# Rows of the modulation spread over partitions by DMA transposes instead of TensorE, in an adaptive-LayerNorm block

## The chip, the cores and the metric

The kernel runs on one core of a Trainium2 chip. The core has five engines with instruction streams of their own: TensorE (PE in the profile, its weight loads PEld), VectorE (DVE), ScalarE (ACT), GpSimd (POOL) and SyncE (SP), which here only issues DMAs. ScalarE and GpSimd issue DMAs too; an issue stands in the engine's stream in program order. The metric is the device time of one execution in microseconds, as a median of several runs.

## What is computed

The reference, cut to what matters. Here D = 1024, the sequence is S = 2048, and the feed-forward width is F = 3584; all inputs are bfloat16.

```python
mod = (_silu(c) @ w_mod).reshape(c.shape[0], 6, 1, -1)   # w_mod is 1024 x 6144
sa, ca, ga, sb, cb, gb = (mod[:, 0], ..., mod[:, 5])      # six rows of 1024
h = _layernorm(x) * (1 + ca) + sa
x = x + ga * _A_ref(h, A_wqkv, A_wo)                      # linear attention, 32 heads
h = _layernorm(x) * (1 + cb) + sb
x = x + gb * _B_ref(h, B_w_gate, B_w_up, B_w_down)        # (silu(h @ w_gate) * (h @ w_up)) @ w_down
```

Two of the six rows, sa and ca, are needed at once. The four others are "late": ga scales the output projection w_o, sb and cb modulate the second LayerNorm, gb scales w_down. The kernel multiplies ga into the columns of w_o and gb into the columns of w_down, in SBUF, so for these two it needs the row of 1024 values repeated on all 128 partitions.

## The kernel before

The stages run one after the other on TensorE: K, V and Q projections with the key-value sums (steps ("K", s, i), ("V", s, i), ("Q", s, i) for four chunks s of 512 rows), then 28 gate/up steps for each of the four chunks (("GU", s, f)), with the attention output of the late rows woven into the first pass, then the down projection (("D", st, h)). A list `seq` holds these steps in order; `put(label, ...)` hangs other work behind a step. The order of the program is the order of each engine's stream.

A step of gate/up, and its rotation through five PSUM banks:

```python
def nextbank():
    b = bank[state["b"]]
    state["b"] = (state["b"] + 1) % 5
    return b

def gu_mm(sc_, f):
    ...
    g_ps = nextbank()
    for cc in range(DC):                       # 8 matmuls of 512 columns
        nc.tensor.matmul(g_ps[:], lhsT=wg_blk[:, cc, fs], rhs=M4[:, sc_, cc, :], ...)
    sg = epool.tile([P, NB], F32, name="e")
    nc.scalar.activation(out=sg[:], in_=g_ps[:], func=ACT.Silu)
    u_ps = nextbank()
    for cc in range(DC):
        nc.tensor.matmul(u_ps[:], lhsT=wu_blk[:, cc, fs], rhs=M4[:, sc_, cc, :], ...)
    nc.vector.tensor_tensor(out=gus[sc_][:, f, :], in0=u_ps[:], in1=sg[:], op=ALU.mult)
```

Weight blocks of gate and up (512 KB each, two steps' worth) come on SyncE's queue into three buffers. During the first pass ScalarE's queue carries the transposes of the attention output and of the normalised rows:

```python
def nd_tr(st):
    nc.scalar.dma_start_transpose(out=oTs[st % 3], in_=os_[st % 2])
def o_tr(st):
    nc.scalar.dma_start_transpose(out=M4[:, sc_, :, t * P:(t + 1) * P], in_=xn2s[st % 3])
```

The late rows ga, cb and sb are made thus: eight transposing loads of w_mod, so that the 1024 columns of a row lie on partitions (128 at a time); eight multiply-and-sum instructions on VectorE against silu(c) spread over all partitions (`sc_bc`); each gives 128 values in one column of `colF`.

```python
def load_late(q, i, js):
    for j in js:
        nc.sync.dma_start_transpose(out=rowT[i][:, j], in_=wm_v[:, j, q * D:(q + 1) * D])
def late_sum(q, i, bs):
    for b in bs:
        nc.vector.tensor_tensor_reduce(out=prod..., in0=rowT[i][:, :, b, :], in1=sc_bc..., ...,
                                       accum_out=colF[:, q, b:b + 1])
```

A result in columns must be turned back into a row on all partitions for silu(c) and for ga: VectorE repeats each column 128 times along the free dimension (`spread`, into `rep`), then TensorE transposes the eight squares and ScalarE copies them out of PSUM:

```python
def late_bc(dst):
    tp = nextbank()[:].bitcast(BF16).rearrange("p (c s) -> p c s", c=DC)
    for cc in range(DC):
        nc.tensor.transpose(tp[:, cc, :], rep[:, cc, :], ident[:])
    nc.scalar.copy(out=dst[:].rearrange("p (c s) -> p c s", c=DC), in_=tp)
```

The row gb is made in another way. Two plain loads bring its part of w_mod in halves of 512 columns; VectorE sums eight slices, weighted by silu(c) as a scalar per partition, splits the float32 sum into two bfloat16 parts, and TensorE sums over partitions with a square of ones, which leaves the row on all partitions at once (`part_sum`, `part_split`, `part_bc`).

Of the kernel before, what the change touches and what calls it, by code (L numbers as in the profile page):

```python
# [9 lines left out]
ALU = mybir.AluOpType  # L10
BF16 = mybir.dt.bfloat16
F32 = mybir.dt.float32
# [9 lines left out]
def kernel(  # L22
# [13 lines left out]
    nc = tc.nc  # L36
    P = nc.NUM_PARTITIONS
    _, S, D = A_x.shape
# [3 lines left out]
    DC = D // P  # L42
# [5 lines left out]
    NB = 512  # L48
    NH = D // NB
    FC = F // P  # L50
# [16 lines left out]
    wm_v = w_mod.rearrange("(p j) n -> p j n", j=DC)  # L67
    c_v = c.rearrange("o (p j) -> p (o j)", j=DC)

    const = ctx.enter_context(tc.tile_pool(name="const", bufs=1))  # L70
# [10 lines left out]
    M3 = const.tile([P, 16384], BF16, name="M3")  # L81
# [5 lines left out]
    def view(region, off, shape, dtype=BF16):  # L87
        n = 1
        for s_ in shape:
            n *= s_  # L90
        w = n * (2 if dtype == F32 else 1)
        ap = region[:, off:off + w]
        if dtype == F32:
            ap = ap.bitcast(F32)
        if len(shape) == 2:
            ap = ap.rearrange("p (a b) -> p a b", a=shape[0])
        elif len(shape) == 3:
            ap = ap.rearrange("p (a b c) -> p a b c", a=shape[0], b=shape[1])
        return ap
# [19 lines left out]
    obs = [view(M6, 4096 + 1024 * i, [D]) for i in range(2)]  # L119
    rowT = [view(M3, 4096, [DC, DC, P]), view(M6, 0, [DC, DC, P])]  # L120
    prod = view(M5, 8256, [D], F32)
    wmg = [view(M3, 4096 * (1 + i), [DC, NB]) for i in range(2)]
    accG = view(M3, 12288, [D], F32)
    hlG = view(M3, 14336, [2, NB])
    xs = [view(M7, 1024 * i, [D]) for i in range(6)]
    xns = [view(M7, 6144 + 1024 * i, [D]) for i in range(6)]
    wgs = [view(M7, 4096 * i, [DC, FBW]) for i in range(3)]
# [2 lines left out]
    def wd(f):  # L130
        return wd_lo[:, f] if f < 14 else wd_hi[:, f - 14]
# [40 lines left out]
    ident = const.tile([P, P], BF16, name="ident")  # L172
# [11 lines left out]
    ga_bc = const.tile([P, D], BF16, name="ga_bc")  # L184
    gb_bc = ga_bc
    KVZ = const.tile([P, HG, KVW], BF16, name="KVZ")
    rep = const.tile([P, DC, P], BF16, name="rep")
    sc_bc = const.tile([P, D], BF16, name="sc_bc")
    colF = const.tile([P, 6, DC], F32, name="colF")
    ones = const.tile([P, P], BF16, name="ones")  # L190
    nc.gpsimd.memset(ones[:], 1.0)
    scF = const.tile([P, DC], F32, name="scF")

    scT = const.tile([P, DC], BF16, name="scT")
    nc.scalar.activation(out=scT[:], in_=c_sb[:], func=ACT.Silu)
    nc.scalar.copy(out=scF[:], in_=scT[:])

    def warm(n):
        for _ in range(n):
# [62 lines left out]
# [4 lines that stand above are left out]
# [54 lines left out]
    GA, SB, CB, GB = 2, 3, 4, 5  # L320

    def load_late(q, i, js):
        for j in js:
            nc.sync.dma_start_transpose(out=rowT[i][:, j], in_=wm_v[:, j, q * D:(q + 1) * D])

    def late_sum(q, i, bs):
        for b in bs:
            nc.vector.tensor_tensor_reduce(out=prod.rearrange("p (j k) -> p j k", j=DC), in0=rowT[i][:, :, b, :],  # L328
                                           in1=sc_bc[:].rearrange("p (j k) -> p j k", j=DC), scale=1.0, scalar=0.0,
                                           op0=ALU.mult, op1=ALU.add, accum_out=colF[:, q, b:b + 1])  # L330

    def late_fin(q):
        if q == SB:
            nc.vector.tensor_copy(out=sbT[:], in_=colF[:, q, :])
        else:
            nc.vector.tensor_copy(out=m1[:, q, :], in_=colF[:, q, :])
            if q == CB:
                nc.vector.tensor_scalar_add(out=cb1T[:], in0=m1[:, q, :], scalar1=1.0)
            else:
                spread(nc.vector, m1[:, q, :])  # L340
# [1 line left out]
    def spread(eng, col):  # L342
        eng.tensor_copy(out=rep[:], in_=col.unsqueeze(2).to_broadcast([P, DC, P]))

    def late_bc(dst):
        tp = nextbank()[:].bitcast(BF16).rearrange("p (c s) -> p c s", c=DC)
        for cc in range(DC):
            nc.tensor.transpose(tp[:, cc, :], rep[:, cc, :], ident[:])  # L348
        nc.scalar.copy(out=dst[:].rearrange("p (c s) -> p c s", c=DC), in_=tp)

    def load_gb(kb):
        k0 = GB * D + kb * NB
        nc.sync.dma_start(out=wmg[kb], in_=wm_v[:, :, k0:k0 + NB])

    def part_sum(kb, js):
        dst = accG[:, kb * NB:(kb + 1) * NB]
        for j in js:
            if j == 0:
                nc.vector.tensor_scalar_mul(out=dst, in0=wmg[kb][:, 0, :], scalar1=scF[:, 0:1])
            else:  # L360
                nc.vector.scalar_tensor_tensor(out=dst, in0=wmg[kb][:, j, :], scalar=scF[:, j:j + 1], in1=dst,  # L361
                                         op0=ALU.mult, op1=ALU.add)

    def part_split(kb):
        src = accG[:, kb * NB:(kb + 1) * NB]
        nc.vector.tensor_copy(out=hlG[:, 0, :], in_=src)
        nc.vector.tensor_tensor(out=hlG[:, 1, :], in0=src, in1=hlG[:, 0, :], op=ALU.subtract)

    def part_bc(kb):
        b = nextbank()  # L370
        for s_ in range(2):
            nc.tensor.matmul(b[:], lhsT=ones[:], rhs=hlG[:, s_, :], start=(s_ == 0), stop=(s_ == 1))
        nc.scalar.copy(out=gb_bc[:, kb * NB:(kb + 1) * NB], in_=b[:])


    def tr0(st):
# [113 lines left out]
    def put(label, *fns):  # L490
        after.setdefault(label, []).extend(fns)
# [156 lines left out]
    put(("K", 1, 7), lambda: [load_x(st) for st in range(12, 16)])  # L648


    put(("V", 0, 5), lambda: late_bc(sc_bc))

    def put_late(q, i, loads, sums):
        for k in range(DC):
            put(loads[k], lambda k=k: load_late(q, i, (k,)))
            put(sums[k], lambda k=k: late_sum(q, i, (k,)))
        put(sums[-1], lambda: late_fin(q))

    put_late(GA, 0, [("Q", 0, k) for k in range(8)], [("V", 1, k) for k in range(8)])
    put(("K", 2, 3), lambda: late_bc(ga_bc))  # L660
    put_late(CB, 1, [("V", 1, k) for k in range(8)], [("V", 2, k) for k in range(8)])
    put(("V", 2, 7), lambda: nc.sync.dma_start(out=wo, in_=wo_v))
    put_late(SB, 0, [("V", 2, k) for k in range(8)], [("V", 3, k) for k in range(8)])
    put(("GU", 0, 18), lambda: load_gb(0), lambda: load_gb(1))
    gb_at = [("GU", 0, f) for f in range(21, FC)] + [("GU", 1, f) for f in range(8)]
    for kb in range(2):
        for k in range(4):
            put(gb_at[5 * kb + k], lambda kb=kb, k=k: part_sum(kb, (2 * k, 2 * k + 1)))
        put(gb_at[5 * kb + 3], lambda kb=kb: part_split(kb))
        put(gb_at[5 * kb + 5], lambda kb=kb: part_bc(kb))  # L670
    for cc in range(DC):
        put(("K", 3, 4 + cc) if cc < 4 else ("V", 3, cc - 4), lambda cc=cc: nc.vector.tensor_tensor(out=wo[:, cc, :], in0=wo[:, cc, :], in1=ga_bc[:],
                                                               op=ALU.mult))
# [41 lines left out]
            range(14 + 4 * (i - 4), min(18 + 4 * (i - 4), FC)) for i in range(8)}  # L715
    for i in range(8):
        for k, f in enumerate(wd_f[i]):
            put(("GU", 1, max(3 * i + 4, 7 + i) + k // 2) if i < 7 else ("GU", 1, FC - 2 + k),
                lambda f=f: nc.vector.tensor_tensor(out=wd(f), in0=wd(f), in1=gb_bc[:], op=ALU.mult))
    put(("GU", 1, FC - 4), lambda: load_x1r(0), lambda: load_x1r(1))  # L720
    for st in range(2, ST):
# [37 lines left out]
```

## Time and profile before

| quantity | value |
|---|---|
| time, median of 3 runs | 840.07 us (839.58 to 840.27) |
| span of the profiled execution | 837.9 us |
| busy: TensorE, VectorE, ScalarE, GpSimd | 827.3, 354.6, 153.2, 79.5 us |
| granted TensorE clock | 1.000 |
| bytes moved by DMA | 128.62 MB |
| transposing DMAs | 32 on ScalarE's queue, 36 on SyncE's |

How to read it: a group's line gives the source line, engine, operation, output and input with shapes, the number of instructions, then busy time, the mean of one in ns, and the idle time of the engine just before. The program's big SBUF regions all appear as M, the PSUM banks as bank; gb_bc is the same memory as ga_bc and bears its name. A windows line gives the stretch, its length, then busy time of PE, PEld, DVE, ACT and POOL with instruction counts, the granted clock, the mean busy share of the 16 DMA engines (over 1 where packets overlap) and GB/s. A timeline line gives start, length, engine, source line and operation; a trailing q on an engine (SPq, ACTq) means its instruction sequencer, as in the issue of a DMA. Busy times of TensorE overlap one another, since its matmuls are pipelined.

### The profile page before, as it was taken

How to read it: one execution, taken by the hardware profiler on the slowest of the kernel's cores; microseconds unless marked ns; L12 is line 12 of the kernel's file. 1: busy time of each engine (PE TensorE's matmuls, PEld its weight loads, DVE VectorE, ACT ScalarE, POOL GpSimd, SP SyncE). 2: the span in 40 equal slices, each digit the busy share in tenths (PEclk: the TensorE clock that was granted, in tenths of full speed). 3: DMA queues.
4: the chain of work that ended last, by engine and by line, in shares of the span. 5: the costliest groups of instructions: out<-in, count | busy, mean ns of one | idle time of the engine just before them, and what ended most of it. 6: DMA issues, size and time to landing. Idle time of an engine off the chain costs nothing.

```text
span 837.9 us, 10535 instructions
## 1 busy us (share of the span) xinstructions
PE 827.3 (99%) x4148; PEld 390.2 (47%) x4228; DVE 354.6 (42%) x662; ACT 153.2 (18%) x289; POOL 79.5 (9%) x147
## 2 busy tenths in 40 slices
PE   8999999999999999999999999999999999999998
PEld 4454544544444444444444444444444444444445
DVE  5758888788656656635342111112101111111111
ACT  3335533323211111111110001111000111100000
POOL 2114300032222223100000000000000000000000
PEclk9999999999999999999999999999999999999999
DMA  9985878154598999787884225555312555211220
GB/s 300 312 180 111 130 175 202 41 136 125 146 216 219 224 231 283 189 251 226 251 248 136 76 70 151 154 153 154 104 70 90 155 152 152 75 37 45 76 70 26
DMA packets 220993, 128.62 MB, mean 154 GB/s; under 512 B 76048, under 2 KB 207120, under 8 KB 220944
## 3 DMA queue, kind: packets, MB, share of 16 engines
q1 hardware_dynamic: 180096, 98.58, 42.9%
q10 hardware_dynamic: 38544, 20.98, 10.9%
q0 software_dynamic: 2304, 8.39, 2.6%
q8 instruction: 33, 0.54, 0.3%
q14 instruction: 16, 0.13, 0.1%
HBM read 97.52 MB, written 12.58 MB: 131 GB/s over the span
## 4 chain that ended last, share of the span: by engine, by line
PE 96%; SPq 2%; DMA 1%; issue 1%; DVE 0%; DVEq 0%
PE bank L576 23%; PE bank L595 23%; PE bank L570 23%; PE bank L527 7%; PE bank L289 7%; PE bank L297 7%; PE bank L274 6%; DMA M<-in_w_mod_dram 1%; PE bank L500 1%; PE bank L306 1%; SPq L147 1%; SPq L150 1%; SPq L140 0%; PE bank L348 0%; DVE M L361 0%
## 5 line engine op out<-in xcount | busy, mean ns | idle before, releaser
L576 PE MATMUL bank<-M,M 128*128 128x512 bf16 x881 | 210.4, 379 | 0.9
L570 PE MATMUL bank<-M,M 128*128 128x512 bf16 x870 | 209.5, 379 | 1.3
L578 DVE TENSOR_TENSOR M<-bank,e 128x512 bf16<-128x512 f32 x112 | 77.4, 691 | 249.8 <-PE bank L576 241.3
L595 PE MATMUL bank<-M,M 128*128 128x512 bf16 (+2 forms) x717 | 147.4, 362 | 0.7
L573 ACT ACTIVATE e<-bank 128x512 f32<-128x512 f32 x112 | 66.8, 598 | 436.2 <-PE bank L570 404.1
L595 PEld LDWEIGHTS <-M 128*128 128x128 bf16 x952 | 90.9, 98 | 103.0
L576 PEld LDWEIGHTS <-M 128*128 128x128 bf16 x896 | 87.7, 98 | 105.7
L570 PEld LDWEIGHTS <-M 128*128 128x128 bf16 x896 | 87.3, 98 | 103.8
L598 DVE TENSOR_TENSOR M<-bank,M 128x512 bf16<-128x512 f32 (+2 forms) x34 | 22.4, 660 | 169.9 <-PE bank L595 169.9
L274 PE MATMUL bank<-M,M 128*128 128x512 bf16 x248 | 56.6, 379 | 1.7 <-DVE M L256 1.0
L527 PE MATMUL bank<-M,M 128*128 128x512 bf16 x254 | 57.8, 379 | 0.1
L297 PE MATMUL bank<-M,M 128*128 128x512 bf16 x250 | 56.7, 379 | 0.3
L289 PE MATMUL bank<-M,M 128*128 128x512 bf16 x251 | 55.8, 379 | 0.3
L269 ACT ACTIVATE e<-bank 128x512 f32<-128x512 f32 x64 | 37.7, 595 | 86.1 <-PE bank L297 49.6
L595 PE MATMUL bank<-M 128*128 128x512 bf16 x218 | 50.3, 379 | 0.2
L271 DVE SCALAR_TENSOR_TENSOR M<-bank,e 128x512 bf16<-128x512 f32 x64 | 44.3, 691 | 3.9
L270 DVE TENSOR_SCALAR e<-e 128x512 f32<-128x512 f32 x64 | 29.4, 460 | 24.9 <-ACT e L269 24.9
L289 PEld LDWEIGHTS <-M 128*128 128x128 bf16 x256 | 25.0, 98 | 30.0
L527 PEld LDWEIGHTS <-M 128*128 128x128 bf16 x256 | 25.0, 98 | 29.7
L274 PEld LDWEIGHTS <-M 128*128 128x128 bf16 x256 | 24.3, 98 | 29.3 <-DVE M L256 1.8
L297 PEld LDWEIGHTS <-M 128*128 128x128 bf16 x256 | 24.6, 98 | 27.9
L328 DVE CUSTOM_DVE_ANT_0 M<-M,sc_bc 128x1024 f32<-128x1024 bf16 x24 | 29.8, 1241 | 0.5
(85 smaller groups left out, 358.2 us busy)
## 6 DMA issues: line engine op xcount, KB each, us to landing
M<-in_B_w_gate_dram SPq DMA_DIRECT2D x56, 512.0 KB, 3.8
M<-in_B_w_up_dram SPq DMA_DIRECT2D x56, 512.0 KB, 4.9
x_scratch<-M POOLq DMA_DIRECT2D x16, 512.0 KB, 5.6
M<-x_scratch ACTq DMA_DIRECT2D x16, 512.0 KB, 3.4
M<-in_B_w_down_dram SPq DMA_DIRECT2D x6, 1024.0 KB, 8.2
M<-in_A_x_dram SPq DMA_DIRECT2D x16, 256.0 KB, 3.9
M<-in_A_wqkv_dram SPq DMA_DIRECT2D x4, 1024.0 KB, 11.4
M<-in_A_x_dram ACTq DMA_DIRECT2D x16, 256.0 KB, 3.8
```

The costliest lines, as they stand in the source:

```text
L269: nc.scalar.activation(out=e[:], in_=acc, func=ACT.Exp)
L271: nc.vector.scalar_tensor_tensor(out=dst, in0=acc, scalar=0.0, in1=e[:], op0=ALU.max, op1=ALU.add)
L274: nc.tensor.matmul(acc[:], lhsT=M4[:, sc_, cc, t * P:(t + 1) * P], rhs=wk[:, cc, h * NB:(h + 1) * NB], start=(cc == 0), stop=(cc == DC - 1))
L289: nc.tensor.matmul(acc[:], lhsT=M4[:, sc_, cc, t * P:(t + 1) * P], rhs=wv[:, cc, h * NB:(h + 1) * NB], start=(cc == 0), stop=(cc == DC - 1))
L297: nc.tensor.matmul(acc[:], lhsT=wq[:, cc, qc * P:(qc + 1) * P], rhs=M4[:, sc_, cc, :], start=(cc == 0), stop=(cc == DC - 1))
L328: nc.vector.tensor_tensor_reduce(out=prod.rearrange("p (j k) -> p j k", j=DC), in0=rowT[i][:, :, b, :], in1=sc_bc[:].rearrange("p (j k) -> ...
L527: nc.tensor.matmul(acc[:], lhsT=oTs[st % 3][:, cc, :], rhs=wo[:, cc, hs], start=(cc == 0), stop=(cc == DC - 1))
L570: nc.tensor.matmul(g_ps[:], lhsT=wg_blk[:, cc, fs], rhs=M4[:, sc_, cc, :], start=(cc == 0), stop=(cc == DC - 1))
L573: nc.scalar.activation(out=sg[:], in_=g_ps[:], func=ACT.Silu)
L576: nc.tensor.matmul(u_ps[:], lhsT=wu_blk[:, cc, fs], rhs=M4[:, sc_, cc, :], start=(cc == 0), stop=(cc == DC - 1))
L578: nc.vector.tensor_tensor(out=gus[sc_][:, f, :], in0=u_ps[:], in1=sg[:], op=ALU.mult)
L595: nc.tensor.matmul(y_ps[:, 0:w], lhsT=gus[sc_][:, f, t * P:(t + 1) * P], rhs=wd(f)[:, c0:c1], start=(f == 0), stop=(f == FC - 1))
```

## The change

Everything that spread rows over partitions by TensorE is done by DMA. `late_bc` becomes a single transposing DMA from `rep` to the destination, SBUF to SBUF, issued by SyncE for silu(c) and ga. The special path of gb goes: gb is now made like the three other late rows, but its eight transposing loads and its spreading are issued on ScalarE's queue, where the transposes of that stage already are. The scaling of w_down by gb moves to later steps of the second gate/up pass, since gb is ready later. The purpose is to free TensorE, PSUM banks and ScalarE's evictions from the work of spreading rows, and to have one way for all late rows.

The diff, cut to its core (`...` marks cuts; the removed buffers wmg, accG, hlG, ones and scF served only the removed path):

```diff
-    ones = const.tile([P, P], BF16, name="ones")
-    nc.gpsimd.memset(ones[:], 1.0)
-    scF = const.tile([P, DC], F32, name="scF")
...
-    nc.scalar.copy(out=scF[:], in_=scT[:])
...
     def load_late(q, i, js):
+        eng = nc.scalar if q == GB else nc.sync
         for j in js:
-            nc.sync.dma_start_transpose(out=rowT[i][:, j], in_=wm_v[:, j, q * D:(q + 1) * D])
+            eng.dma_start_transpose(out=rowT[i][:, j], in_=wm_v[:, j, q * D:(q + 1) * D])
...
-    def late_bc(dst):
-        tp = nextbank()[:].bitcast(BF16).rearrange("p (c s) -> p c s", c=DC)
-        for cc in range(DC):
-            nc.tensor.transpose(tp[:, cc, :], rep[:, cc, :], ident[:])
-        nc.scalar.copy(out=dst[:].rearrange("p (c s) -> p c s", c=DC), in_=tp)
-
-    def load_gb(kb):
-        k0 = GB * D + kb * NB
-        nc.sync.dma_start(out=wmg[kb], in_=wm_v[:, :, k0:k0 + NB])
-
-    def part_sum(kb, js):
-        dst = accG[:, kb * NB:(kb + 1) * NB]
-        for j in js:
-            ...        # 8 multiply-adds of 128x512 on VectorE, by scF[:, j:j + 1]
-    def part_split(kb):
-        ...            # a bfloat16 copy and the rest, on VectorE
-    def part_bc(kb):
-        b = nextbank()
-        for s_ in range(2):
-            nc.tensor.matmul(b[:], lhsT=ones[:], rhs=hlG[:, s_, :], start=(s_ == 0), stop=(s_ == 1))
-        nc.scalar.copy(out=gb_bc[:, kb * NB:(kb + 1) * NB], in_=b[:])
+    def late_bc(eng, dst):
+        eng.dma_start_transpose(out=dst[:].rearrange("p (c s) -> p c s", c=DC),
+                                in_=rep[:].rearrange("p c s -> p (c s)"))
...
-    put(("V", 0, 5), lambda: late_bc(sc_bc))
+    put(("V", 0, 5), lambda: late_bc(nc.sync, sc_bc))
...
-    put(("K", 2, 3), lambda: late_bc(ga_bc))
+    put(("K", 2, 3), lambda: late_bc(nc.sync, ga_bc))
...
-    put(("GU", 0, 18), lambda: load_gb(0), lambda: load_gb(1))
-    gb_at = [("GU", 0, f) for f in range(21, FC)] + [("GU", 1, f) for f in range(8)]
-    for kb in range(2):
-        ...            # part_sum, part_split, part_bc put at gb_at[5 * kb + k]
+    put_late(GB, 0, [("GU", 0, 22 + k) if k < 6 else ("GU", 1, k - 6) for k in range(8)], [("GU", 1, 2 + k) for k in range(8)])
+    put(("GU", 1, 10), lambda: late_bc(nc.scalar, gb_bc))
...
-            put(("GU", 1, max(3 * i + 4, 7 + i) + k // 2) if i < 7 else ("GU", 1, FC - 2 + k),
+            put(("GU", 1, (12, 14, 16, 18, 19, 21, 23)[i] + k // 2) if i < 7 else ("GU", 1, FC - 2 + k),
                 lambda f=f: nc.vector.tensor_tensor(out=wd(f), in0=wd(f), in1=gb_bc[:], op=ALU.mult))
```

More of the change, by code (lines that the diff above doesn't have):

```diff
@@ L121 @@
     prod = view(M5, 8256, [D], F32)
-    wmg = [view(M3, 4096 * (1 + i), [DC, NB]) for i in range(2)]
-    accG = view(M3, 12288, [D], F32)
-    hlG = view(M3, 14336, [2, NB])
     xs = [view(M7, 1024 * i, [D]) for i in range(6)]
@@ L343, in spread @@
         eng.tensor_copy(out=rep[:], in_=col.unsqueeze(2).to_broadcast([P, DC, P]))
-    def late_bc(dst):
-        tp = nextbank()[:].bitcast(BF16).rearrange("p (c s) -> p c s", c=DC)
-        for cc in range(DC):
-            nc.tensor.transpose(tp[:, cc, :], rep[:, cc, :], ident[:])
-        nc.scalar.copy(out=dst[:].rearrange("p (c s) -> p c s", c=DC), in_=tp)
-    def load_gb(kb):
-        k0 = GB * D + kb * NB
-        nc.sync.dma_start(out=wmg[kb], in_=wm_v[:, :, k0:k0 + NB])
-    def part_sum(kb, js):
-        dst = accG[:, kb * NB:(kb + 1) * NB]
-        for j in js:
[L358 to L362, printed above, removed]
-    def part_split(kb):
-        src = accG[:, kb * NB:(kb + 1) * NB]
-        nc.vector.tensor_copy(out=hlG[:, 0, :], in_=src)
-        nc.vector.tensor_tensor(out=hlG[:, 1, :], in0=src, in1=hlG[:, 0, :], op=ALU.subtract)
-    def part_bc(kb):
-        b = nextbank()
-        for s_ in range(2):
-            nc.tensor.matmul(b[:], lhsT=ones[:], rhs=hlG[:, s_, :], start=(s_ == 0), stop=(s_ == 1))
-        nc.scalar.copy(out=gb_bc[:, kb * NB:(kb + 1) * NB], in_=b[:])
+    def late_bc(eng, dst):
+        eng.dma_start_transpose(out=dst[:].rearrange("p (c s) -> p c s", c=DC),
+                                in_=rep[:].rearrange("p c s -> p (c s)"))
     def tr0(st):
@@ L663 @@
     put_late(SB, 0, [("V", 2, k) for k in range(8)], [("V", 3, k) for k in range(8)])
-    put(("GU", 0, 18), lambda: load_gb(0), lambda: load_gb(1))
-    gb_at = [("GU", 0, f) for f in range(21, FC)] + [("GU", 1, f) for f in range(8)]
-    for kb in range(2):
[L667 to L670, printed above, removed]
+    put_late(GB, 0, [("GU", 0, 22 + k) if k < 6 else ("GU", 1, k - 6) for k in range(8)], [("GU", 1, 2 + k) for k in range(8)])
+    put(("GU", 1, 10), lambda: late_bc(nc.scalar, gb_bc))
     for cc in range(DC):
```

## Prediction

> **What bounds the kernel now.** I read the page from the top: the busy shares, then the chain of work that ended last, then TensorE's busy time in three long stretches of the windows view.
>
> ```profile
> PE 827.3 (99%) x4148; PEld 390.2 (47%) x4228; DVE 354.6 (42%) x662; ACT 153.2 (18%) x289; POOL 79.5 (9%) x147
> ...
> PE 96%; SPq 2%; DMA 1%; issue 1%; DVE 0%; DVEq 0%
> ...
> 0.00:24.00 24.00, 20.71 (x211) 11.12 (x215) 11.59 (x34) 7.25 (x8) 5.41 (x27) 1.00 0.97 308
> 24.00:448.00 424.00, 421.46 (x2132) 200.66 (x2171) 280.56 (x536) 112.45 (x225) 74.05 (x120) 1.00 0.76 194
> 448.00:838.00 390.00, 385.16 (x1814) 178.39 (x1847) 62.45 (x92) 33.48 (x56) 0.00 (x0) 1.00 0.33 100
> ```
>
> The first line says that TensorE is busy 99% of the span, the second that 96% of the closing chain is TensorE work. A busy share alone would not settle it, since matmuls overlap in the record. The Trainium skill, "Perfetto Trace Analysis", section "Identifying the Most-Contended Engine", warns of just that and points to the weight loads instead; here weight loads are busy only 47%, so that number alone would suggest slack. The pitch of the matmuls decides: eight matmuls of a bank start 1.73 us apart from the next eight in the timeline of the gate/up stage, 0.216 us each, for 512 columns, over and over, at a granted clock of 1.00. And when I ask the waits view for TensorE alone, from 25 us to the end, it lists no wait at all. Only the first 24 us have gaps (20.71 of 24.00 us busy), where the chain runs through the first loads of w_mod and wqkv. So after 24 us **the instruction stream of TensorE is the time**: what is taken out of it shortens the run by its slot, and what is done on another engine costs nothing until TensorE must wait for it.
>
> **What the change takes out of TensorE.** The timeline shows the slots. What counts is the start of the group's first weight load to the start of the next group's, not the durations.
>
> ```profile
> 41.00 0.65 PEld L348 LDWEIGHTS <-rep 128*128 128x128 bf16 x8
> ...
> 41.61 2.31 PEld L289 LDWEIGHTS <-M 128*128 128x128 bf16 x12
> ...
> 364.40 0.31 PEld L372 LDWEIGHTS <-ones 128*128 128x128 bf16 x2
> ...
> 364.83 1.61 PEld L570 LDWEIGHTS <-M 128*128 128x128 bf16 x8
> ```
>
> Eight transposes of rep hold TensorE from 41.00 to 41.61: 0.61 us. The second spreading, at 96.88 to 97.49, is the same 0.61. The two matmuls against ones for one half of gb hold it from 364.40 to 364.83: 0.43 us, and the other half from 346.70 to 347.13 too. In all 2 x 0.61 + 2 x 0.43 = **2.08 us**. The Trainium skill has a figure for the transposes ("TensorE: Matmul & The Clock Gate", section "Part 4: PE-mode transpose": about 390 ns in isolation, about 275 ns within a kernel). Sixteen by that would be 4.4 to 6.2 us; the trace gives 219 ns for one and a pitch of 76 ns in the run of eight, so I use the trace.
>
> **What else goes and comes.** ScalarE loses two evictions of 1.02 us and two of 0.585 us (3.2 us), VectorE the partial sums of gb: 14 x 0.747 + 2 x 0.476 + 2 x 0.426 + 2 x 0.693 = 13.7 us. VectorE gains eight sums of 128x1024 at 1.24 + 0.08 us, one column copy (0.17) and one spread of rep (0.69): 11.4 us. Both lie beside TensorE. The ones memset and the scF copy (0.20 us each) lie at 1.32 and 4.05 us on POOL and ScalarE; POOL then idles 2.78 us for VectorE, and ScalarE 2.16 us for POOL, so neither is on the way. The scaling of w_down keeps its 28 x 0.68 us of VectorE and only moves to later slots, still inside the second gate/up pass, while the first w_down matmul stands at about 448 us.
>
> The two big plain loads of w_mod (2 x 1 MB at 305.7 us, 10.6 and 15.0 us to landing) go. In their place ScalarE's queue issues eight transposing loads of 256 KB, one per gate/up step from step 22 of the first pass (about 326 to 360 us), and one spreading. SyncE's queue gets two spreadings. What such a load costs is seen where the earlier rows are loaded by SyncE:
>
> ```profile
> 50.33 12.06 SPq L324 DMA_TRANSPOSE M<-in_w_mod_dram  x8
> ...
> 52.00:56.00 4.00, 3.95 (x20) 1.77 (x19) 3.29 (x9) 1.43 (x3) 0.00 (x0) 1.00 1.00 222
> 56.00:60.00 4.00, 4.00 (x20) 1.86 (x19) 3.93 (x10) 1.55 (x3) 0.00 (x0) 1.00 0.95 179
> ...
> L324 SPq DMA_TRANSPOSE M<-in_w_mod_dram x24: 1232/1308/4452, 50.3 to 120.9; - x24
> ...
> DMA to landing us min/median/max: 3.9/4.3/9.1
> ```
>
> Eight take 12.06 us of issue with the DMA engines full (the last columns of a windows line are clock, DMA share and GB/s), so each is about 1.5 us of all DMA engines, and holds its issuing engine 1.3 us as a rule and 4.45 us at worst. The Trainium skill ("DMA: Bandwidth & Descriptors", section "Issuing engines are not separate DMA queues") says that the issuing engine saves only issue time and that all queues share 16 DMA engines; so ScalarE's queue buys order against the other transposes on that queue, not bandwidth. The section "Silent corruption: two transposing streams in flight at once" of the same page of the Trainium skill asks that one queue's transposes wait for the other's. That would be a wait, but SyncE's last transpose is issued at 120.9 and landed by 130 us, and ScalarE's first is at 161.3 us; the new spreadings on SyncE (41 and 97 us) and the gb loads on ScalarE keep this split.
>
> On SyncE the first spreading stands behind four transposes of x and ahead of plain loads, 1.23 us of issue like its neighbours; the sums that need it begin at 77 us, 30 us later. The second stands between two transposes of x at about 100 us; w_o is scaled with it some 30 us later. Both hidden.
>
> **Rivals.** First, *ScalarE is held up by issuing*. One gate/up step is 3.45 us and ScalarE has one activation of 0.60 us in it, so 2.85 us are free. At 1.3 us per issue this fits twice; at 4.6 us, as one transpose in the saturated stretch took, it doesn't:
>
> ```profile
> 310.27 4.61 ACTq L546 DMA_TRANSPOSE M<-M  x1
> ...
> 340.00:344.00 4.00, 4.00 (x20) 1.86 (x19) 3.49 (x6) 0.60 (x1) 0.00 (x0) 1.00 1.10 273
> 344.00:348.00 4.00, 4.00 (x21) 1.77 (x19) 1.24 (x3) 1.05 (x2) 0.00 (x0) 1.00 0.78 218
> 348.00:352.00 4.00, 3.95 (x19) 1.86 (x19) 3.96 (x11) 0.73 (x2) 0.00 (x0) 1.00 0.42 112
> ```
>
> TensorE turns through five banks, 1.73 us a group, so a bank comes back four groups, 6.9 us, after it is full; less 0.6 us of eviction, about 6.3 us of lateness are free, and the 4.61 us issue above cost TensorE nothing. If all eight took 4.6 us, each would be 1.75 us over its step: 14 us of lateness, about 8 us lost. But the DMA share from 340 to 356 us is 0.42 to 1.10, mean 0.71, and eight loads at 1.5 us per 3.45 us add 0.43: near full, not beyond the 1.16 seen at 320 to 332 us with no wait of TensorE. I give a visible stall one chance in eight, typically 1 to 4 us.
>
> Second, *VectorE waits for a landing*. Each gb sum reads all eight loads; the last is issued after the activation of step 1 of the second pass, near 358 us, and with 4.3 to 9.1 us to landing arrives at 362 to 367 us, beside 1 MB of w_down. The first sum stands behind the product at 362 us: a wait of 0 to 5 us against about 6.2 us free. Likewise the last transposed tile of the hidden rows now queues behind three gb loads; in the kernel before, it was issued at 338.5 and used at 349 us. Probably hidden.
>
> Third, *the weights come late*: gate and up blocks of 1 MB per 6.9 us land in 3.8 to 4.9 us at the median, and are asked for two blocks (13.8 us) ahead. Landing would have to triple. Removing the two 1 MB loads even eases 305 to 324 us. Against it.
>
> Fourth, *a gain beyond the slots*, were the DMA or VectorE a hidden limit now: the empty list of TensorE waits speaks against it.
>
> **Range and chances.** 840.07 - 2.08 = 838.0 us, a ratio of 0.9975. Runs of the kernel before spread 0.7 us. Downward I allow that and a little: 837.2. Upward, one stall of 1.5 to 2 us eats the gain: 839.8. Two per cent is 16.8 us, twice the whole-backlog case, so nearly all chance is within it.
>
> **What would show it.** Right: TensorE has 20 fewer instructions and the gate/up, Q/K/V and down stages keep their pitch; the span falls by about 2 us, half of it by 100 us and half by 365 us; TensorE still lists no wait after 25 us; the issues on ScalarE's queue take 1.3 to 3 us. Wrong: TensorE waits for activations or products between 326 and 395 us, with issues of 4 us or more (first rival); VectorE idle until a w_mod landing (second); a weight-load wait for gate or up blocks (third); or a changed opening before 24 us, which my sum leaves untouched.

## The result and the profile after

The changed kernel takes 837.89 us (median of 6 runs, 837.63 to 838.31) against 840.1 us for the kernel before in the same series, a ratio of 0.9973 with a 95% interval of [0.996, 0.9986]. It was measured again later, beside one of the experiments: 838.12 against 839.81 us, 0.9977 [0.9967, 0.9986]. So the gain is about 2 us, and it is there.

The page of the changed kernel, its busy shares and the engines of the chain that ended last, and then the windows view of the two long stretches behind the opening (columns: stretch, its length, busy time of PE, PEld, DVE, ACT and POOL, clock, DMA share, GB/s):

```profile
PE 829.2 (99%) x4208; PEld 388.7 (46%) x4208; DVE 351.3 (42%) x660; ACT 149.9 (18%) x284; POOL 79.2 (9%) x146
...
PE 97%; SPq 2%; DMA 1%; issue 0%; DVE 0%
```

```profile
24.00:446.00 422.00, 421.68 (x2152) 199.25 (x2149) 277.20 (x534) 109.42 (x221) 74.06 (x120) 1.00 0.78 196
446.00:836.00 390.00, 387.23 (x1850) 178.49 (x1848) 62.44 (x92) 33.43 (x56) 0.00 (x0) 1.00 0.34 100
```

The picture has not changed: TensorE is the chain, and its waits view from 25 us to the end is as empty as before. One trap lies in the first line. TensorE's busy time went *up*, 827.3 to 829.2 us, though it has 20 instructions less to do. The weight loads tell the truth: 4228 became 4208, exactly 20 fewer. The matmul records of the kernel before were incomplete (its gate matmuls are listed as 870, the changed kernel's as 896, which is 112 groups of eight), and where records are missing, the busy time is too small. A busy time with records missing can't judge a gain of 2 us.

A better ruler is the distance between two marks that both kernels have: the first weight load of a V projection in the opening, and the first of the down projection. Here are the two marks in the kernel before and in the changed kernel, each from the view of one source line (durations min/median/max in ns, then first and last start in us):

```profile
L289 PEld LDWEIGHTS <-M x256: 97/98/98, 30.6 to 147.3; 128*128 128x128 bf16 x128
L595 PEld LDWEIGHTS <-M x952: 97/98/98, 447.7 to 834.7; 128*128 128x128 bf16 x191
```

```profile
L282 PEld LDWEIGHTS <-M x256: 97/98/98, 30.6 to 146.4; 128*128 128x128 bf16 x128
L563 PEld LDWEIGHTS <-M x952: 97/98/98, 445.9 to 833.0; 128*128 128x128 bf16 x191
```

From 30.6 to 447.7 us is 417.1 us before; from 30.6 to 445.9 us is 415.3 us after: **1.8 us** less. The last weight load of the V projections, at 147.3 against 146.4 us, splits it: 0.9 us by then, where only the two spreadings differ, and another 0.9 us by the second mark, where only gb differs. In what follows this distance is called the stretch; the marks are given to 0.1 us.

### The profile page after: what moved, and what is told of

Same layout as the page of the kernel before. It is cut to its first block, busy times and chain, and to the rows that moved or that the text cites. A ratio compares the mean times of both kernels' runs of the same rounds, so it can differ in the third digit from the quotient of the medians.

```text
span 836.1 us, 10576 instructions
## 1 busy us (share of the span) xinstructions
PE 829.2 (99%) x4208; PEld 388.7 (46%) x4208; DVE 351.3 (42%) x660; ACT 149.9 (18%) x284; POOL 79.2 (9%) x146
## 4 chain that ended last, share of the span: by engine, by line
PE 97%; SPq 2%; DMA 1%; issue 0%; DVE 0%
PE bank L563 23%; PE bank L538 23%; PE bank L544 23%; PE bank L282 7%; PE bank L495 7%; PE bank L290 7%; PE bank L267 6%; DMA M<-in_w_mod_dram 1%; SPq L144 1%; PE bank L468 1%; PE bank L299 1%; SPq L147 0%; SPq L137 0%; PE bank L363 0%; DVE M L566 0%
## 5 line engine op out<-in xcount | busy, mean ns | idle before, releaser
L322 DVE CUSTOM_DVE_ANT_0 M<-M,sc_bc 128x1024 f32<-128x1024 bf16 x32 | 40.0, 1249 | 0.5
L282 PEld LDWEIGHTS <-M 128*128 128x128 bf16 x256 | 25.0, 98 | 30.2
```

Of the source, the lines that this page charges most:

```text
L282: nc.tensor.matmul(acc[:], lhsT=M4[:, sc_, cc, t * P:(t + 1) * P], rhs=wv[:, cc, h * NB:(h + 1) * NB], start=(cc == 0), stop=(cc == DC - 1))
```

## The experiments

Three theories stood behind the expectations. Theory A: TensorE's stream is the time, and what an instruction costs there is read from the start of one group's matmuls to the start of the next's. Theory B: the same, with slots read from the weight loads, as the prediction did. Theory C: the gain comes from relief of the DMA engines or VectorE on the new path of gb. All stretches found:

| kernel | marks, us | stretch | time, us | ratio to before [95%] |
|---|---|---|---|---|
| before | 30.6, 447.7 | 417.1 | 840.07 | |
| changed | 30.6, 445.9 | 415.3 | 837.89 | 0.9973 [0.996, 0.9986] |
| spreadings only | 32.6, 448.8 | 416.2 | 838.94 | 0.9987 [0.9979, 0.9995] |
| gb only | 30.2, 446.4 | 416.2 | 839.08 | 0.9988 [0.998, 0.9996] |
| spreadings eightfold on TensorE | 30.3, 453.6 | 423.3 | 846.39 | 1.0073 [1.0059, 1.0088] |
| gb loads two a step | 30.8, 449.2 | 418.4 | 838.67 | 0.9989 [0.9976, 1.0001] |
| gb loads all at once | 30.6, 458.5 | 427.9 | 849.96 | 1.0114 [1.0097, 1.0131] |
| gb on SyncE's queue | 30.9, 451.5 | 420.6 | 839.67 | 1.0005 [0.9994, 1.0017] |
| opening filled | 30.5, 445.9 | 415.4 | 838.04 | 0.9978 [0.9968, 0.9987] |
| changed, again | 31.2, 446.5 | 415.3 | 838.12 | 0.9977 [0.9967, 0.9986] |

Marks and stretch are of the one profiled execution, the time is the median of all, and each ratio is to runs of the kernel before in the same series.

### The two spreadings alone

```diff
 (the kernel before, with)
-    def late_bc(dst):   # eight TensorE transposes and a ScalarE copy
+    def late_bc(eng, dst):   # one transposing DMA
-    put(("V", 0, 5), lambda: late_bc(sc_bc))
+    put(("V", 0, 5), lambda: late_bc(nc.sync, sc_bc))
-    put(("K", 2, 3), lambda: late_bc(ga_bc))
+    put(("K", 2, 3), lambda: late_bc(nc.sync, ga_bc))
```

> The kernel before, with only the two spreadings of silu(c) and ga done by DMA; gb keeps its ones matmuls. Theory A (the time is TensorE's stream, and a slot is read from matmul start to matmul start: 41.22 to 41.66 us, 0.44 us for eight transposes): the first w_down weight load, at 447.7 us before and 445.9 in the changed kernel, comes 0.9 us earlier than before (446.8), time 839.2. Theory B (slots read from weight loads, 0.61 us each, as predicted): 1.2 us earlier. Theory C (the gain is relief of DMA or VectorE by the new gb path): no gain at all here, 0 to 0.2 us.

The time was 838.94 us, 0.9 us below the 839.83 us of before in this series. In the profiled execution everything came 2 us late from the opening on (the clock was halved there; the last section shows it), so the bare position of the second mark says nothing and the stretch has to be taken: 416.2 us, 0.9 us below before. That is theory A's number, and theory C's nothing is out. Against theory B's 1.2 us speaks the stretch alone, with marks given to 0.1 us; the interval of the ratio, a gain of 0.4 to 1.8 us, holds both.

### gb alone

```diff
 (the changed kernel, with TensorE's late_bc kept as pe_bc)
-    put(("V", 0, 5), lambda: late_bc(nc.sync, sc_bc))
+    put(("V", 0, 5), lambda: pe_bc(sc_bc))
-    put(("K", 2, 3), lambda: late_bc(nc.sync, ga_bc))
+    put(("K", 2, 3), lambda: pe_bc(ga_bc))
```

> The changed kernel with the two spreadings put back on TensorE; only gb goes the new way. Theory A: the first w_down weight load comes 0.86 us earlier than before (446.8 to 446.9 us), and together with the run that has the spreadings alone it makes up the whole 1.8 us. Theory B also says 0.86 here. Theory C: nearly the whole 1.8 us is found here.

839.08 us, 0.75 us below before. The second mark came at 446.4 us, but the first came 0.4 us early as well; the stretch is 416.2 us, again 0.9 us shorter. The two halves add up: 0.9 + 0.9 = 1.8 us, the whole of the change. Within the 0.1 us to which the marks are given, nothing is left over for an interaction of the two, or for theory C.

### The spreadings eightfold

```diff
 (the kernel before, with)
     def late_bc(dst):
         ...
-        for cc in range(DC):
+        for cc in list(range(DC)) * 8:
             nc.tensor.transpose(tp[:, cc, :], rep[:, cc, :], ident[:])
```

> The kernel before, with each of the two spreadings' eight transposes done eight times over into the same bank (14 times eight more than before, the row is the same). Theory A (0.44 us per eight): 14 x 0.44 = 6.2 us more than before, 846.3 us. Theory B (0.61 us per eight): 14 x 0.61 = 8.5 us, 848.6 us. If TensorE's stream were not the time (theory C), much less than 6 us would show.

This magnifies the disputed term. The time was 846.39 us against 839.83, 6.6 us more; the interval of the ratio, 0.59% to 0.88%, is 5.0 to 7.4 us and leaves theory B's 8.5 us out. The stretch grew by 6.2 us (423.3 - 417.1) for 14 additional groups: **0.443 us for eight transposes**, 55 ns each. So one more TensorE transpose in this stream costs 55 ns. It isn't the 219 ns of its record, and not the 76 ns that the weight loads of one short run suggested. TensorE's timeline shows where the 76 came from; here are the weight loads, then the matmuls, of the first group of 64:

```profile
40.66 3.77 PEld L348 LDWEIGHTS <-rep 128*128 128x128 bf16 x64
44.40 3.17 PEld L289 LDWEIGHTS <-M 128*128 128x128 bf16 x16
...
40.88 3.74 PE L348 MATMUL bank<-ident,rep 128*128 128x128 bf16 x64
44.45 3.62 PE L289 MATMUL bank<-M,M 128*128 128x512 bf16 x15
```

By the weight loads the group takes 44.40 - 40.66 = 3.74 us, by the matmuls 44.45 - 40.88 = 3.57 us. The difference is 0.17 us, the same as for eight (0.61 against 0.44). So the weight loads are wrong by a fixed amount per group, which spread over only eight transposes looks like a dearer transpose. The eightfold run alone gives the cost of each further transpose; that nothing fixed comes on top for a whole group is shown by the run with the spreadings alone, 0.9 us for two.

### Bunching the gb loads on ScalarE

The first rival of the prediction was that ScalarE, held up by issuing loads, is late with its activations until TensorE has no free bank. In the changed kernel that didn't happen. Two kernels push it there: two loads a step, and all eight at once.

```diff
 (the changed kernel; gb loads, two a step)
-    put_late(GB, 0, [("GU", 0, 22 + k) if k < 6 else ("GU", 1, k - 6) for k in range(8)], ...)
+    put_late(GB, 0, [("GU", 0, 25 + k // 2) if k < 6 else ("GU", 1, 0) for k in range(8)], ...)
 (all at once)
+    put_late(GB, 0, [("GU", 0, 25) for k in range(8)], ...)
```

> The changed kernel with the eight gb loads bunched, two in each of four gate/up steps (25 to 27 of the first pass and 0 of the second) instead of one in each of eight. At 1.9 us an issue, the median in the changed kernel, two take 3.8 us against 2.85 us that ScalarE has free in a step: 0.95 us late per step, some 4 us after four, inside the 6.3 us that five banks allow: no wait of TensorE, 837.9 us. If issues slow to 4 us because the DMA engines are full, 5 us late per step, some 20 us after four: TensorE loses 10 us or more, about 850 us. I expect the middle: 0 to 3 us lost.

> The changed kernel with all eight gb loads issued one after the other behind step 25 of the first gate/up pass. SyncE issued eight such loads in 12 to 13 us earlier in the kernel, with little else on the DMA engines; here the gate and up weights run beside them, so 13 to 20 us. ScalarE does no activation in that time. If ScalarE's issuing only costs once lateness passes the slack of the banks, 6.3 us less what it had: TensorE stalls 7 to 14 us, and the time is 845 to 852 us. If ScalarE's lateness never reaches TensorE (the slack is larger than I think): 837.9. If every us of issue counts: 13 to 20 us more than the changed kernel.

All at once first. The timeline of ScalarE, then of TensorE, with the windows of that time (clock, DMA share and GB/s in the last three columns):

```profile
341.80 0.60 ACT L541 ACTIVATE e<-bank 128x512 f32<-128x512 f32 x1 [2.86 <-PE bank L538]
341.80 18.80 ACTq L318 DMA_TRANSPOSE M<-in_w_mod_dram  x8
360.70 1.57 ACT L541 ACTIVATE e<-bank 128x512 f32<-128x512 f32 x3 [18.30 <-DMA M<-in_w_mod_dram]
...
361.35 3.57 PE L544 MATMUL bank<-M,M 128*128 128x512 bf16 x8 [9.23 <-ACT e L541]
364.71 2.69 PE L538 MATMUL bank<-M,M 128*128 128x512 bf16 x8
...
356.00:360.00 4.00, 0.00 (x0) 0.00 (x0) 0.00 (x0) 0.00 (x0) 0.00 (x0) 0.51 1.23 270
360.00:364.00 4.00, 2.65 (x7) 0.98 (x7) 2.67 (x8) 1.57 (x3) 0.00 (x0) 0.50 0.60 118
364.00:368.00 4.00, 4.00 (x15) 1.53 (x14) 1.82 (x4) 0.56 (x1) 0.00 (x0) 0.71 0.00 0
```

The issues hold ScalarE for 18.80 us. The next activation was due one step of 3.45 us after 341.80, at 345.25, and began at 360.70: 15.45 us late. TensorE stood for 9.23 us. The difference, **6.2 us**, is the lateness that five banks absorb; the prediction had worked out 6.3. The three activations at once at 360.70 are the backlog. The stretch is 12.6 us longer than the changed kernel's, and the starts of the groups split that. 0.8 us was lost ahead of any gb load: the first matmul of the output projection starts at 168.51 us against 167.74. The standstill is 9.4 us: the group due 1.73 us after 350.23 us starts at 361.35. The remaining 2.4 us follow the standstill: the granted clock is half, eight matmuls take 3.57 us instead of 1.89, two groups take 5.90 us (361.35 to 367.25) instead of 3.45, and the clock is back at 1.00 in the window from 368 us. The time, 849.96 us, lies within the 845 to 852 that the first case had expected.

With two loads a step the profiled execution (at 841.07 us one of the longer ones) shows the same arithmetic near its threshold:

```profile
341.19 5.59 ACTq L318 DMA_TRANSPOSE M<-in_w_mod_dram  x2
346.91 4.35 ACTq L318 DMA_TRANSPOSE M<-in_w_mod_dram  x2
351.39 5.25 ACTq L318 DMA_TRANSPOSE M<-in_w_mod_dram  x2
356.77 6.21 ACTq L318 DMA_TRANSPOSE M<-in_w_mod_dram  x2
363.08 1.57 ACT L541 ACTIVATE e<-bank 128x512 f32<-128x512 f32 x3 [5.74 <-issue]
```

Four pairs take 21.4 us, where four steps have 13.8. The activation at 363.08 was due at 341.19 + 4 x 3.45 = 355.0 us, so it is 8.1 us late; less 6.2 us that leaves 1.9 us, and 1.9 us is the wait of TensorE for an activation that the waits view lists (a second one, 0.9 us, follows for a product). This kernel is on the edge: its runs range from 837.58 us, as short as the changed kernel, to 842.34 us. Its interval reaches 1.0001, so against the kernel before the medians alone decide nothing; the wait in the trace does.

### The gb loads on SyncE's queue

```diff
 (the changed kernel, with)
-        eng = nc.scalar if q == GB else nc.sync
+        eng = nc.sync
-    put(("GU", 1, 10), lambda: late_bc(nc.scalar, gb_bc))
+    put(("GU", 1, 10), lambda: late_bc(nc.sync, gb_bc))
```

> The changed kernel with the gb loads and the gb spreading on SyncE's queue instead of ScalarE's. The two queues' transposes must now wait for each other's landing: the gb loads wait for the last transposes of the hidden rows, and those wait for gb loads, with the gate and up weights behind the loads on SyncE. If the choice of queue matters for time (rival): ScalarE is held for a landing of 5 to 9 us, SyncE asks for weights 5 to 10 us late, and TensorE stalls for 1 to 5 us: 839 to 843 us. If all of this fits in the slack of the five banks (6.3 us) and of the three weight buffers (9 us): 837.9, the same as the changed kernel, with longer waits on ScalarE and SyncE in the trace and none on TensorE.

839.67 us, and the gain over before is gone: 1.0005 [0.9994, 1.0017]. The runs range from 839.03 to 843.44 us, and the profiled execution is the longest of them, so its waits show the kind of the loss and not its usual size. SyncE's timeline, then its waits (us in total, times, longest), then ScalarE's timeline and TensorE's only wait of any size after the opening:

```profile
326.35 16.00 SPq L318 DMA_TRANSPOSE M<-in_w_mod_dram  x2
...
SPq L318 <- DMA M<-M: 16.9, 2, 11.0
...
349.57 1.25 ACTq L514 DMA_TRANSPOSE M<-M  x1
350.92 1.57 ACT L541 ACTIVATE e<-bank 128x512 f32<-128x512 f32 x3 [11.93 <-issue]
...
PE bank L544 <- ACT e L541: 3.4, 1, 3.4
```

The transposing loads on SyncE and the transposes of the hidden rows on ScalarE now take turns: SyncE waits 16.9 us for landings of ScalarE's transposes (M<-M), and ScalarE in its turn is held ahead of its transpose until 349.57 us, so that three activations pile up and TensorE waits 3.4 us. (The view of the gb loads' line names ScalarE's activation among those who waited for them, once, 11.9 us.) This is what the Trainium skill, "DMA: Bandwidth & Descriptors", asks for in its section "Silent corruption: two transposing streams in flight at once", seen as time: the stream that comes later waits for the earlier one's landing. The gate and up weights, behind the loads on SyncE, never made TensorE wait. With all of gb on ScalarE there is one stream in that stage, and no such wait.

### The opening filled, and the changed kernel again

```diff
 (the changed kernel, with)
+    def fill(n):
+        for _ in range(n):    # adds zero to a bank in use
+            nc.tensor.matmul(bank[3][:], lhsT=zt[:, 0:P], rhs=zt, start=False, stop=False, ...)
...
     kblk(range(3, 7), 4)
+    fill(2)
     mod_mm(2, 0, 4, 8)
+    fill(2)
     mod_mm(2, 1, 4, 8)
+    fill(2)
```

> The changed kernel with six matmuls of zeros added into a bank in use (they add zero), in three pairs between 21.9 and 24.6 us, where TensorE waits for the last parts of w_mod. In the run with the spreadings alone the granted clock was 0.50 from 26 to 28 us after such a wait and everything later came 2 us later; in the kernel before and the changed kernel it stayed at 1.00. If short idle stretches in the opening decide whether the clock is halved there, the filled kernel never shows it: the same median as the changed kernel within 0.3 us (837.6 to 838.1), and no run above 839. If the halving has another cause, some runs still lie 1.5 to 2.5 us above the lowest, as with the kernel before. If the filling delays the matmuls that wait, up to 0.6 us more in all runs.

> The changed kernel itself on the same chip as the filled one, in more rounds. TensorE's stream is shorter by 2 x 0.44 + 2 x 0.43 = 1.74 us (matmul start to matmul start), so the ratio to the kernel before is 0.9979 if both meet the halved clock of the opening equally often; the earlier measurement was 0.9973 [0.996, 0.9986]. If the DMA path has a benefit of its own beyond TensorE's slots, it is below 0.9970.

The filled kernel took 838.04 us (837.68 to 838.87), the changed one in the same series 838.12 us (837.63 to 838.42). TensorE's waits after 20 us were gone from the filled kernel's list, while the changed one had a wait of 0.7 and one of 0.3 us there; the time is the same. And since the changed kernel didn't show the halved clock of the opening in any of these runs either, whether filling prevents it was not tested: inconclusive. The second measurement of the changed kernel, 0.9977, is where theory A put it (0.9979); its interval begins at 0.9967, so a small benefit beyond the slots isn't excluded by it.

## Why the prediction was right, and where a term was off

**The bound and the direction** held. TensorE waits for nothing after 25 us in either kernel, and each piece taken out of its stream shortened the run by its own slot, half by the spreadings and half by gb, as the prediction had it.

**The sum** was 2.08 us; the slots come to 1.74 us, the stretch shows 1.8. The mis-sized term is the transposes: 2 x 0.61 us in the prediction, 2 x 0.44 in the runs. The step that failed is the sentence that the start of the group's first weight load to the start of the next group's counts. A weight load starts ahead of its matmul, and not always by the same time: by 0.22 us for the first transpose (41.00 against 41.22 us), which follows a matmul of 512 columns, and by only 0.05 us for the first matmul behind the group (41.61 against 41.66 us), which follows a short one. The 0.17 us between the two went into the predicted slot. The matmul starts of the same stretch, in the timeline of TensorE in the kernel before, and the changed kernel's counterpart:

```profile
36.68 4.70 PE L289 MATMUL bank<-M,M 128*128 128x512 bf16 x20
41.22 0.61 PE L348 MATMUL bank<-ident,rep 128*128 128x128 bf16 x8
41.66 3.62 PE L289 MATMUL bank<-M,M 128*128 128x512 bf16 x16
45.12 1.07 PE L306 MATMUL bank<-M 128*128 128x129 bf16 x16
```

```profile
36.66 8.15 PE L282 MATMUL bank<-M,M 128*128 128x512 bf16 x37
44.65 1.07 PE L299 MATMUL bank<-M 128*128 128x129 bf16 x16
```

From 41.22 to 41.66 us is 0.44 us, and the next stage comes 45.12 - 44.65 = 0.47 us earlier, of which 0.02 us was there already at the start. For matmuls of full width both readings agree (346.92 to 347.35 and 346.70 to 347.13: 0.43 us), so that term was right. The time moved by 2.2 us in one series and 1.7 us in another; both intervals hold 1.74 and 2.08. So it was the traces and the eightfold run, not the result, that told the two apart, and that the first series came within 0.1 us of the predicted 838.0 is luck: 840.07 - 1.74 is 838.3.

**The work beside TensorE** was sized rightly enough. ScalarE's busy time fell by 3.3 us (3.2 predicted for the evictions), VectorE's by 3.3 us (2.3 predicted), and none of it shows in the time.

**The first rival**, ScalarE held up by issuing, came near. Lines of ScalarE's timeline in the changed kernel:

```profile
342.96 0.60 ACT L541 ACTIVATE e<-bank 128x512 f32<-128x512 f32 x1 [4.79 <-PE bank L544]
...
345.19 0.60 ACT L541 ACTIVATE e<-bank 128x512 f32<-128x512 f32 x1 [1.63 <-PE bank L538]
345.22 4.12 ACTq L318 DMA_TRANSPOSE M<-in_w_mod_dram  x1
349.44 0.60 ACT L541 ACTIVATE e<-bank 128x512 f32<-128x512 f32 x1 [3.65 <-issue]
```

The eight issues took 1.25 to 4.12 us, median 1.9, where 1.3 to 3 us had been expected. An activation at 337.57 us was on time, so in steps of 3.45 us the next three were due at 341.0, 344.5 and 347.9 us; they began at 342.96, 345.19 and 349.44, which is 1.9, 0.7 and 1.5 us late, out of the 6.2 us that are free. The first of these delays is a gb issue of 1.96 us with a transpose of the hidden rows behind it, 3.22 us; the last is the issue of 4.12 us. The DMA share between 340 and 360 us rose to 1.23 from 0.68, more than the added 0.43 worked out. Spreading the loads one to a step is what kept this harmless, as bunching showed.

**The second rival**, VectorE waiting for a landing, was there in one of its two forms: VectorE waited 1.53 us for the last transposed tile of the hidden rows (at 348.50 us), behind the gb loads, as foreseen; the first gb sum waited for no load. Nothing of it reached TensorE. **The third** (late weights) did not come: no wait of TensorE for weights, even with them behind the gb loads on SyncE. Nor did **the fourth** (a gain beyond the slots): none is left over when the halves are added, to 0.1 us.

## What to carry to other kernels

When one engine's stream is the time, price what you take out of it from matmul start to matmul start, and check a small term by multiplying it as well as by removing it: the first gives the cost of one more, the second that of the whole group. Work moved to another engine's queue is free only as long as its issue time, multiplied by how bunched it is, stays within the lateness that the buffers absorb: here 6.2 us as measured, or 6.3 us as four groups of 1.73 us less one eviction, with the loads spread one to a step. And put transposing DMAs of one stage on one queue: on two they took turns here, and the waits held up the activations that stood behind them.

## What was not expected of the hardware

An idle TensorE costs more than the idling. After the standstill of 9.23 us the granted clock was 0.5 from about 356 us on and 0.71 on average from 364 to 368 us, which added 2.4 us to it. The wait of 3.4 us with gb on SyncE's queue was followed by a slow clock too; after the 1.9 us with two loads a step the clock stayed at 1.00 (the windows behind the two waits, in this order):

```profile
352.00:356.00 4.00, 4.00 (x11) 1.51 (x11) 4.00 (x11) 0.50 (x2) 0.00 (x0) 0.57 0.41 78
364.00:368.00 4.00, 4.00 (x20) 1.79 (x19) 1.00 (x2) 1.25 (x3) 0.00 (x0) 1.00 1.16 265
```

The same halving shows in some executions right in the opening. In the profiled one of the kernel with the spreadings only, TensorE waited 0.74 and 0.32 us near 24 and 25 us; the windows view has

```profile
24.00:28.00 4.00, 3.54 (x21) 1.54 (x22) 2.03 (x7) 0.00 (x0) 0.00 (x0) 0.66 1.09 359
```

a clock of 0.66 on average over four microseconds, and all that follows comes 2 us later. The changed kernel waited as long there when measured again (0.74 and 0.32 us) and kept its full clock, so the waits alone don't decide it; what does stays open.
